# Reused bytes waited for tile by tile, and six row buffers instead of five

## The chip, the cores and the metric

The kernel runs on one core of one Trainium2 chip. The metric is device time of one execution in microseconds (us): 1251.45 before the change, the median of three runs (1250.16 to 1252.48). The core has five engines with a queue each, worked off in order: PE (TensorE, matmuls), DVE (VectorE), ACT (ScalarE), POOL (GpSimd) and SP (SyncE, which here only issues DMAs; POOL issues some too).

## The reference, cut to what matters

Attention over 4 batches, 8 heads, 576 tokens and a head width of 64, in which each query keeps its 32 largest scores; then a layer of eight experts (MoE), to which a token goes only if its skip score is positive, and there to one expert; then a gated layer over all 2304 tokens.

```
scores = q @ k.T / 8                       # 576 x 576 for each of 32 heads
kth = 32nd largest of each row;  scores = where(scores >= kth, scores, -1e9)
attn = softmax(scores) @ v                 # -> x, 2304 tokens x 512
do = x @ w_skip > 0                        # the tokens that are computed
e = argmax(x @ w_gate); p = softmax(x @ w_gate)[e]          # 8 experts
x[do] += p * (relu(x @ w1[e]) @ w2[e])     # w1: 512 x 1024, w2: 1024 x 512
g = x @ w_gate2;  v = x @ w_val            # 512 x 1536 each
out = (g * sigmoid(g) * v) @ w_out         # 1536 x 512
```

## The kernel before, in words

The four batches are worked in two groups of two (1152 tokens each). While the attention of the second group runs on DVE (MAX8 and MATCH_REPLACE find the 32 largest) and PE, the experts and the first part of the gated layer of the first group are mixed in. The attention's end at some 780 us is followed by the second group's experts, `moe1(1)`, mixed with the rest of the first group's gated layer `moe2(0)`, and at the end stands the gated layer of the second group, `moe2(1)`.

fp32 products are made of three matmuls on numbers split in a high and a low half. For the experts of the second group, `wsplit` loads 128x1024 weights (512 KB) into a buffer `wraw` (L947, on SP), ACT copies the high half into a buffer `whl` (L950), DVE subtracts it for the low half (L951), and PE multiplies three times (L1014 to L1016 for the first matrix of an expert, L1042 to L1044 for the second). Four `wraw` and six `whl` buffers go round (`Ring`). A row block of an expert is gathered from the rows `xa` by its list of indices (L960, a DMA of POOL) into a buffer `io`, turned on PE (L989), copied and split by ACT (L992) and DVE (L993), and behind the last output matmul added up and scattered back (L967). The result of the first matrix goes through ACT (`hn`, L1019) and is turned on PE again (L1025).

A gated block takes 384 tokens. For each of 12 units it needs 24 matmuls (L1146 to L1148); ACT and DVE or POOL make the gate of it (L1154 to L1158). Then 108 output matmuls follow (L1169 to L1171) into three banks of PSUM, which ACT copies to `io` buffers (L1175) from which SP stores them (L1177). Its weights come in split form from a scratch tensor `w2s` (L1108, POOL) or raw and are split on the fly (`wfly`: L1111 on SP, L1114 on ACT, L1115 on DVE or POOL). At a block's start three `io` buffers are loaded with rows (L1126) and turned (L1129), and split by ACT (L1131) and DVE (L1132).

The order on each engine is that in which a scheduler places the instructions of the program: it goes by the tiles' dependences, by the number of buffers of a name and by its own costs. Memory is handed out by pools, stacked from two sides. Two places matter here. At some 306 us the pool of the routing and first attention of group 0 closes, and `Moe`'s pools "moe" and "pm" open in its bytes; the first load there is L580, of gated weights into an `h2h` buffer, which DVE (L610 to L612) and others work on. At some 780 us `sa.close()` ends the attention's pools, and "moe2", "pm2" and "ring2" open in theirs; the first load there is L947. The routing of the second group ends with matmuls L547, which ACT copies (L550), and whose result gives the index lists.

The `Moe` object of the second pair has as its last argument the number of `io` buffers, 5, 128x512 floats each. They serve the gathers of `moe1(1)`, then the row loads and output copies of `moe2(1)`. The output copies of the first group's blocks have two `io` buffers of their own.

Of the kernel before, what the change touches and what calls it, by code (L numbers as in the profile page):

```python
# [32 lines left out]
class Kernel:  # L33
# [15 lines left out]
        self.constants()  # L49

    def pool(self, stack, name, side="left"):
        return stack.enter_context(self.tc.tile_pool(name=name, bufs=1, side=side))

    def psum_pool(self, stack, name, side="left"):
        return stack.enter_context(self.tc.tile_pool(name=name, bufs=1, side=side, space=bass.MemoryType.PSUM))

    def constants(self):
        nc, c = self.nc, self.const
# [388 lines left out]
    def rbank(self):  # L447
        if self.rps:
            pool, name, n = self.rps
            return pool.tile([P, 512], F32, name=name, bufs=n)  # L450
        return self.ps.tile([P, 512], F32, name="pT", bufs=3)
# [162 lines left out]
    def run(self):  # L614
        nc = self.nc
        with ExitStack() as st:
# [69 lines left out]
            while m1 and next(m1, None) is not None:  # L686
                pass
            sa.close()
            mp = Moe(self, self.pool(st, "moe2", "right"), self.psum_pool(st, "pm2", "right"), 5,
                     Ring(self.pool(st, "ring2", "right"), 4, 6), 5)  # L690
            n1 = mp.moe1(1, [nc.vector])
            while done2 < cost2 + PRE:
                done2 += next(m2)
# [232 lines left out]
class Moe:  # L926
    def __init__(self, k, pool, psum, nm, ring, nio):
        self.k, self.mo, self.nio = k, pool, nio
        self.ring = ring
        self.pm = self.po = psum  # L930
        self.nm = self.no = nm
        self.fly = None
        self.fresh = []
        self.io = pool
# [286 lines left out]
```

## Time and profile before

| | |
|---|---|
| median of three runs | 1251.45 us |
| the profiled execution: its own time | 1253.92 us |
| its span (first to last instruction) | 1252.1 us |
| PE busy | 1171.3 us, 94% |
| DVE busy | 987.5 us, 79% |
| ACT busy | 734.1 us, 59% |
| POOL busy | 595.0 us, 48% |
| mean granted clock of PE | 0.975 |

The profile is one execution. Busy time is a sum over the span; where an engine waits is seen in its timeline, which gives for each instruction its start, its length and, in brackets, the idle time before it with the event that ended it. The windows give busy times of stretches of 25 us.

### The profile page before, as it was taken

What the parts mean: (1) busy time and instruction counts of PE and PEld (TensorE: products, weight loads), DVE (VectorE), ACT (ScalarE), POOL (GpSimd) and SP (SyncE); (2) the same over time, 40 slices, a digit from 0 to 9 for tenths busy, and PEclk for the clock granted to TensorE, in tenths of its full rate; (3) what the DMA queues carried; (4) which work ended last, traced back from release to release, by engine and by line L of the source; (5) the groups of instructions that cost most, each with busy time, mean ns of one, the idle gap of its engine ahead of it and who ended that gap; (6) DMA issues with size and microseconds to landing.
All of it is one profiled execution on the core that took longest, in us unless ns stands there. A gap on an engine that the chain in (4) does not pass through costs nothing.

```text
span 1252.1 us, 21503 instructions
## 1 busy us (share of the span) xinstructions
PE 1171.3 (94%) x7253; PEld 1011.3 (81%) x7254; DVE 987.5 (79%) x2366; ACT 734.1 (59%) x1582; POOL 595.0 (48%) x770
## 2 busy tenths in 40 slices
PE   6999889999999999999988899889999999999995
PEld 5777777887687778878976798789988799898994
DVE  6999999999899999999999963168878257183670
ACT  5989888998655556555564533056766334343430
POOL 6778867887233435333562433212212535555540
PEclk9999999999798999999999999999999989999998
DMA  2023611111187988965756876778987534533520
GB/s 68 25 74 118 223 39 39 39 39 39 61 297 231 316 303 307 295 211 171 247 196 227 283 242 198 262 268 287 295 278 245 177 105 133 169 118 120 158 68 28
DMA packets 136797, 219.11 MB, mean 175 GB/s; under 512 B 37861, under 2 KB 95205, under 8 KB 130405
## 3 DMA queue, kind: packets, MB, share of 16 engines
q1 hardware_dynamic: 129652, 178.86, 43.7%
q0 software_dynamic: 7024, 38.78, 9.4%
q8 instruction: 59, 0.97, 0.3%
q14 instruction: 62, 0.50, 0.1%
HBM read 177.77 MB, written 41.95 MB: 175 GB/s over the span
## 4 chain that ended last, share of the span: by engine, by line
PE 43%; DVE 26%; DMA 9%; issue 4%; ACT 4%; POOL 1%; SPq 0%; ACTq 0%; DVEq 0%; POOLq 0%
PE m L1146 7%; PE m L1147 7%; PE m L1148 7%; DVE tops L255 7%; DVE rest L254 6%; DMA wraw<-in_moe_w_dram 5%; PE m L1092 3%; PE m L1170 3%; PE m L1171 3%; PE m L1169 2%; PE m L1079 2%; PE pT L290 2%; DVE whl L951 2%; PE pT L276 2%; PE pS L207 2%
## 5 line engine op out<-in xcount | busy, mean ns | idle before, releaser
L255 DVE MAX8 tops<-rest 128x8 f32<-128x288 f32 (+1 forms) x432 | 229.8, 546 | 1.6
L1146 PE MATMUL m<-x2h,whl 128*128 128x384 f32 x576 | 198.5, 346 | 11.7 <-ACT io L1175 7.0
L1147 PE MATMUL m<-x2l,whl 128*128 128x384 f32 x576 | 196.6, 341 | 0.9 <-DVE x2l L1132 0.9
L1148 PE MATMUL m<-x2h,whl 128*128 128x384 f32 x576 | 196.0, 341 | 0.0
L1115 POOL TENSOR_TENSOR whl<-wfly,whl 128x1024 fp32r<-128x1024 f32 x54 | 130.1, 2410 | 116.3 <-ACT whl L1114 116.3
L1114 ACT ACTIVATE whl<-wfly 128x1024 fp32r<-128x1024 f32 x69 | 73.1, 1061 | 110.8 <-PE m L1148 65.3
L278 ACT ACTIVATE pt<-pT 128x512 f32<-128x512 f32 (+2 forms) x320 | 113.6, 405 | 41.3 <-PE pT L276 39.8
L254 DVE MATCH_REPLACE8 rest<-tops,rest 128x288 f32<-128x288 f32 x288 | 125.8, 438 | 0.0
L1146 PEld LDWEIGHTS m<-x2h,whl 128*128 128x128 f32 x576 | 109.9, 191 | 14.9 <-ACT io L1175 7.8
L276 PE MATMUL pT<-idn,pp 128*128 128x128 f32 (+1 forms) x720 | 115.1, 284 | 6.3 <-DVE pp L259 4.8
L951 DVE TENSOR_TENSOR whl<-wraw,whl 128x1024 fp32r<-128x1024 f32 x64 | 82.4, 1304 | 39.8 <-ACT whl L950 32.3
L1147 PEld LDWEIGHTS m<-x2l,whl 128*128 128x128 f32 x576 | 109.7, 190 | 1.8 <-DVE x2l L1132 1.2
L1148 PEld LDWEIGHTS m<-x2h,whl 128*128 128x128 f32 x576 | 109.3, 190 | 0.4 <-issue 0.2
L217 ACT ACTIVATE sc<-pS 128x576 f32<-128x576 f32 x144 | 93.5, 649 | 23.8 <-PE pS L207 18.4
L207 PE MATMUL pS<-kT,qT 128*128 128x288 f32 x512 | 104.9, 326 | 2.6 <-ACT sc L217 1.0
L1158 DVE TENSOR_TENSOR h2l<-th,h2h 128x384 fp32r<-128x384 f32 x36 | 86.3, 2396 | 23.9 <-ACT h2h L1157 23.9
L1158 POOL TENSOR_TENSOR h2l<-th,h2h 128x384 fp32r<-128x384 f32 x36 | 45.7, 1270 | 112.8 <-ACT h2h L1157 112.7
L276 PEld LDWEIGHTS pT<-idn,pp 128*128 128x128 f32 (+1 forms) x720 | 83.3, 140 | 17.4 <-issue 10.8
L950 ACT ACTIVATE whl<-wraw 128x1024 fp32r<-128x1024 f32 x64 | 66.8, 1056 | 48.0 <-DMA wraw<-in_moe_w_dram 40.9
L1155 DVE SCALAR_TENSOR_TENSOR th<-th,m 128x384 f32<-128x384 f32 x72 | 39.1, 543 | 68.7 <-ACT th L1154 68.7
L1169 PE MATMUL m<-whl,h2h 128*128 128x512 f32 x216 | 85.7, 401 | 0.8 <-ACT whl L589 0.8
L290 PE MATMUL pT<-pt,vv 128*64 128x256 f32 (+1 forms) x512 | 81.7, 437 | 5.0 <-ACT pt L278 4.9
(205 smaller groups left out, 2935.3 us busy)
## 6 DMA issues: line engine op xcount, KB each, us to landing
wfly<-w2s SPq DMA_DIRECT2D x69, 512.0 KB, 3.6
whl<-in_moe_w_dram SPq DMA_DIRECT2D x32, 1024.0 KB, 7.7
wraw<-in_moe_w_dram SPq DMA_DIRECT2D x64, 512.0 KB, 5.0
whl<-w2s POOLq DMA_DIRECT2D x31, 1024.0 KB, 5.5
w2s<-h2h SPq DMA_DIRECT2D x8, 1024.0 KB, 6.2
w2s<-whl SPq DMA_DIRECT2D x8, 1024.0 KB, 11.0
io<-xa SPq DMA_DIRECT2D x18, 256.0 KB
out_dram<-io SPq DMA_DIRECT2D x18, 256.0 KB, 2.0
```

What stands on the lines that cost most here:

```text
L207: m = self.nc.tensor.matmul(pS[:, x, :W], l, r[:, x * W:(x + 1) * W], start=(n == 0), stop=stop and n == len(ops) - 1)
L254: self.mark = nc.vector.match_replace(hj, h[:, (j - 1) * 8:j * 8], hi if j == 1 else hj, NEG)
L255: nc.vector.max(h[:, j * 8:(j + 1) * 8], hj if j < 3 else rest.rearrange("p a b -> p (a b)"))
L276: self.anchor = nc.tensor.transpose(p[:k, c - a, :], pp[:, c * P:c * P + k], self.idn)
L278: nc.scalar.activation(T[:k, a:z, do:do + n], p[:k, :z - a, so:so + n], AF.Copy)
L951: lo_engine.tensor_tensor(lo, raw, hi.bitcast(F32), op=OP.subtract)
L1115: self.fly_engine.tensor_tensor(lo, raw, hi.bitcast(F32), op=OP.subtract)
L1146: nc.tensor.matmul(pz, wh[:, z, k, :], xh[:, k, :], start=(k == 0), stop=False)
L1147: nc.tensor.matmul(pz, wh[:, z, k, :], xl[:, k, :], start=False, stop=False)
L1148: nc.tensor.matmul(pz, wl[:, z, k, :], xh[:, k, :], start=False, stop=(k == 3))
L1158: lo_engine.tensor_tensor(hl[:, f, :], th, hh[:, f, :].bitcast(F32), op=OP.subtract)
L1169: nc.tensor.matmul(po[t], hh[:, f, s], wh[:, k, :], start=(f == 0), stop=False)
```

## The change

Both helper functions that make pools get an argument: `reuse_waits="tile"`. Without it, the first instruction that uses bytes of a closed pool waits for all that used that pool; with it, for those that used the tiles whose bytes it takes. And the second `Moe` object has six `io` buffers instead of five. The new line in the second helper moves every later line number by one: L947 before is L948 after.

```
--- before.py
+++ after.py
@@ -49,10 +49,11 @@
         self.constants()
 
     def pool(self, stack, name, side="left"):
-        return stack.enter_context(self.tc.tile_pool(name=name, bufs=1, side=side))
+        return stack.enter_context(self.tc.tile_pool(name=name, bufs=1, side=side, reuse_waits="tile"))
 
     def psum_pool(self, stack, name, side="left"):
-        return stack.enter_context(self.tc.tile_pool(name=name, bufs=1, side=side, space=bass.MemoryType.PSUM))
+        return stack.enter_context(self.tc.tile_pool(name=name, bufs=1, side=side, space=bass.MemoryType.PSUM,
+                                                     reuse_waits="tile"))
 
     def constants(self):
         nc, c = self.nc, self.const
@@ -687,7 +688,7 @@
                 pass
             sa.close()
             mp = Moe(self, self.pool(st, "moe2", "right"), self.psum_pool(st, "pm2", "right"), 5,
-                     Ring(self.pool(st, "ring2", "right"), 4, 6), 5)
+                     Ring(self.pool(st, "ring2", "right"), 4, 6), 6)
             n1 = mp.moe1(1, [nc.vector])
             while done2 < cost2 + PRE:
                 done2 += next(m2)
```

With the argument alone the order of instructions is unchanged on every engine, and only waits differ. SP at the second pair of pools, before (`wraw`, `wfly`: weight loads; the names in brackets are what is waited for, DMAHW a lane of DMAs):

```order
L947 DMA wraw<-in_moe_w_dram 128x4x256 [waits DMAHW3_49,DMAHW1_49,DMAHW6_49,DMAHW0_49,DMAHW7_49,PE_49,Pool_49]
L1111 DMA wfly<-w2s 128x1024 [waits DMAHW5_49]
L947 DMA wraw<-in_moe_w_dram 128x4x256 x3
L1111 DMA wfly<-w2s 128x1024
L1111 DMA wfly<-w2s 128x1024 [waits DMAHW2_49]
L947 DMA wraw<-in_moe_w_dram 128x2x512 [waits DMAHW4_49,DVE_49]
L947 DMA wraw<-in_moe_w_dram 128x2x512 [waits DMAHW6_49,DVE_49]
```

and after:

```order
L948 DMA wraw<-in_moe_w_dram 128x4x256
L1112 DMA wfly<-w2s 128x1024 [waits DMAHW5_49]
L948 DMA wraw<-in_moe_w_dram 128x4x256 [waits DMAHW6_49]
L948 DMA wraw<-in_moe_w_dram 128x4x256 [waits DMAHW7_49]
L948 DMA wraw<-in_moe_w_dram 128x4x256 [waits DMAHW0_49]
L1112 DMA wfly<-w2s 128x1024 [waits DMAHW1_49]
L1112 DMA wfly<-w2s 128x1024 [waits DMAHW2_49]
L948 DMA wraw<-in_moe_w_dram 128x2x512 [waits DMAHW4_49,DMAHW3_49,DVE_49]
L948 DMA wraw<-in_moe_w_dram 128x2x512 [waits DMAHW6_49,DVE_49]
```

The order is the same; the first load lost its waits for PE, POOL and five lanes, and the next loads got waits for one lane each.

The sixth buffer moves instructions behind the second pair of pools. SP at the end of the experts, before (`io<-xa`: row loads of a gated block; `out_dram<-io`: stores of outputs):

```order
L1111 DMA wfly<-w2s 128x1024 x4
L1126 DMA io<-xa_214 128x512 x3
L1111 DMA wfly<-w2s 128x1024 x2
L1126 DMA io<-xa_214 128x512
L1111 DMA wfly<-w2s 128x1024
L1126 DMA io<-xa_214 128x512
L1111 DMA wfly<-w2s 128x1024
L1177 DMA out_dram<-io 128x512 x2
L1126 DMA io<-xa_214 128x512
L1177 DMA out_dram<-io 128x512
```

and after:

```order
L1112 DMA wfly<-w2s 128x1024 x5
L1127 DMA io<-xa_214 128x512 x3
L1112 DMA wfly<-w2s 128x1024
L1127 DMA io<-xa_214 128x512 x3
L1112 DMA wfly<-w2s 128x1024 x2
L1178 DMA out_dram<-io 128x512 x3
```

The six row loads stand three and three, all ahead of the first store, and one `wfly` load has moved ahead of the first three.

PE at the second matrix of the first of these experts, before (L1042 to L1044: that matrix; L1146 to L1148: the gated layer):

```order
L1148 MATMUL m<-x2h,whl 128x384
L1043 MATMUL m<-whl,hh 128x512
L1044 MATMUL m<-whl,hl 128x512
L1042 MATMUL m<-whl,hh 128x512
L1043 MATMUL m<-whl,hh 128x512
L1044 MATMUL m<-whl,hl 128x512
L1042 MATMUL m<-whl,hh 128x512
L1043 MATMUL m<-whl,hh 128x512
L1044 MATMUL m<-whl,hl 128x512
L1042 MATMUL m<-whl,hh 128x512
L1146 MATMUL m<-x2h,whl 128x384
L1147 MATMUL m<-x2l,whl 128x384
```

and after:

```order
L1149 MATMUL m<-x2h,whl 128x384
L1044 MATMUL m<-whl,hh 128x512
L1045 MATMUL m<-whl,hl 128x512
L1147 MATMUL m<-x2h,whl 128x384
L1148 MATMUL m<-x2l,whl 128x384
L1149 MATMUL m<-x2h,whl 128x384
L1147 MATMUL m<-x2h,whl 128x384
L1148 MATMUL m<-x2l,whl 128x384
L1149 MATMUL m<-x2h,whl 128x384
L1147 MATMUL m<-x2h,whl 128x384
L1148 MATMUL m<-x2l,whl 128x384
L1149 MATMUL m<-x2h,whl 128x384
```

Twelve gated matmuls have moved ahead of seven matmuls of the expert. On POOL six gathers (L960) stand in a row at the start of these experts instead of five, ahead of the same two `whl` loads, and the one that stood behind the first scatter is gone from there.

## Rows read from the trace of the kernel before

**Rows 1.** Windows: from:to, us, busy (x) of PE PEld DVE ACT POOL, clock, DMA share, GB/s.
```profile
775.00:800.00 25.00, 22.68 (x130) 18.91 (x129) 7.81 (x48) 2.75 (x8) 6.41 (x10) 0.93 0.58 193
800.00:825.00 25.00, 17.12 (x79) 14.47 (x78) 8.09 (x9) 8.25 (x11) 3.70 (x5) 0.86 1.03 361
...
850.00:875.00 25.00, 25.00 (x165) 23.85 (x164) 22.09 (x24) 16.98 (x24) 6.17 (x4) 1.00 0.89 290
```

**Rows 2.** Timeline of PE, 807 to 824: start, length, engine, line, operation, [idle before].
```profile
807.71 0.60 PE L989 MATMUL m<-idn,io 128*128 128x128 f32 x4
812.98 0.69 PE L1146 MATMUL m<-x2h,whl 128*128 128x384 f32 x1 [4.67 <-ACT io L1175]
...
816.66 0.52 PE L1148 MATMUL m<-x2h,whl 128*128 128x384 f32 x1
819.55 0.44 PE L1146 MATMUL m<-x2h,whl 128*128 128x384 f32 x1 [2.37 <-ACT io L1175]
...
821.57 0.34 PE L1148 MATMUL m<-x2h,whl 128*128 128x384 f32 x1
...
823.50 0.39 PE L1016 MATMUL m<-whl,xg 128*128 128x256 f32 x1 [0.82 <-DVE xg L993]
```

**Rows 3.** Timeline of ACT, 795 to 821.
```profile
795.77 0.18 ACT L550 ACTIVATE r_first<-pT 128x16 f32<-128x16 f32 x1 [13.54 <-PE pT L547]
802.04 1.06 ACT L950 ACTIVATE whl<-wraw 128x1024 fp32r<-128x1024 f32 x1 [6.08 <-DMA wraw<-in_moe_w_dram]
811.38 1.06 ACT L950 ACTIVATE whl<-wraw 128x1024 fp32r<-128x1024 f32 x1 [8.28 <-DMA wraw<-in_moe_w_dram]
812.35 0.58 ACT L1175 ACTIVATE io<-m 128x512 f32<-128x512 f32 x1
817.96 1.06 ACT L950 ACTIVATE whl<-wraw 128x1024 fp32r<-128x1024 f32 x1 [5.03 <-DMA wraw<-in_moe_w_dram]
...
820.35 1.05 ACT L950 ACTIVATE whl<-wraw 128x1024 fp32r<-128x1024 f32 x1
```

**Rows 4.** Timeline of SP, 778 to 800: DMAs it issues.
```profile
778.81 0.57 SPq L434 DMA_DIRECT2D xa<-x  x1
795.80 0.39 SPq L947 DMA_DIRECT2D wraw<-in_moe_w_dram  x1
...
796.79 2.62 SPq L947 DMA_DIRECT2D wraw<-in_moe_w_dram  x3
```

**Rows 5.** Waits of SP, 775 to 824: us in total, times, longest.
```profile
SPq L947 <- PE pT L547: 13.3, 1, 13.3
```

**Rows 6.** Timeline of DVE, 803 to 823.
```profile
803.13 1.23 DVE L951 TENSOR_TENSOR whl<-wraw,whl 128x1024 fp32r<-128x1024 f32 x1 [6.90 <-DMA wfly<-w2s]
...
822.76 0.68 DVE L993 TENSOR_TENSOR xg<-m,xg 128x512 fp32r<-128x512 f32 x1
```

**Rows 7.** Timelines of ACT and PE, 950 to 953.
```profile
950.89 1.06 ACT L950 ACTIVATE whl<-wraw 128x1024 fp32r<-128x1024 f32 x1 [4.66 <-DMA wraw<-in_moe_w_dram]
...
952.49 0.66 PE L1025 MATMUL m<-idn,hn 128*128 128x128 f32 x4 [1.56 <-ACT hn L1019]
```

**Rows 8.** Waits of SP, 300 to 345.
```profile
SPq L580 <- PE pT L276: 28.6, 1, 28.6
```

**Rows 9.** Timelines of ACT and DVE near 342.
```profile
342.31 0.66 ACT L217 ACTIVATE sc<-pS 128x576 f32<-128x576 f32 x1
...
343.00 1.36 DVE L610 TENSOR_SCALAR h2h<-h2h 128x1024 int32<-128x1024 int32 x1 [2.38 <-PE pT L300]
```

**Rows 10.** Timeline of POOL near 803.
```profile
803.14 0.61 POOL L1108 DMA_DIRECT2D whl<-w2s  x1
```

**Rows 11.** Timelines of SP, ACT and PE, 998 to 1005.
```profile
998.94 0.86 SPq L1177 DMA_DIRECT2D out_dram<-io  x2
...
1003.26 0.60 ACT L1175 ACTIVATE io<-m 128x512 f32<-128x512 f32 x1 [3.31 <-DMA out_dram<-io]
...
1004.40 1.01 PE L1146 MATMUL m<-x2h,whl 128*128 128x384 f32 x2 [4.70 <-ACT x2h L1131]
```

More of the change, by code (lines that the diff above doesn't have):

```diff
@@ L51, in pool @@
     def pool(self, stack, name, side="left"):
-        return stack.enter_context(self.tc.tile_pool(name=name, bufs=1, side=side))
+        return stack.enter_context(self.tc.tile_pool(name=name, bufs=1, side=side, reuse_waits="tile"))
     def psum_pool(self, stack, name, side="left"):
-        return stack.enter_context(self.tc.tile_pool(name=name, bufs=1, side=side, space=bass.MemoryType.PSUM))
+        return stack.enter_context(self.tc.tile_pool(name=name, bufs=1, side=side, space=bass.MemoryType.PSUM,
+                                                     reuse_waits="tile"))
     def constants(self):
@@ L689, in run @@
             mp = Moe(self, self.pool(st, "moe2", "right"), self.psum_pool(st, "pm2", "right"), 5,
-                     Ring(self.pool(st, "ring2", "right"), 4, 6), 5)
+                     Ring(self.pool(st, "ring2", "right"), 4, 6), 6)
             n1 = mp.moe1(1, [nc.vector])
```

## The prediction

> **What bounds the kernel now.** I read the 25 us windows first, then the engines' timelines in the windows where TensorE (PE) is not full, then the waits of SP's queue, whose loads stand at the start of those gaps. In most windows of the second half PE is busy for all of its 25 us at a granted clock of 1.00 (850 to 875 in [rows 1]); nothing but less PE work or less waiting helps there. The exception is 800 to 825: PE busy 17.12, clock 0.86, while the DMA share is 1.03 at 361 GB/s, after a window with 193 GB/s [rows 1]. Here the second group's experts begin. In [rows 2] the reader is to see PE end the gated output at 807.71 and a turn of 0.60, then stand idle for 4.67 until ACT's copy L1175, run twelve gated matmuls whose starts lie 3.68 us apart first to last (812.98 to 816.66), wait 2.37 for the next copy, run twelve in 2.02 (819.55 to 821.57), and wait 0.82 for DVE's L993 before the first L1016 at 823.50. [Rows 3] say why: the copy at 812.35 stands in ACT's order behind the split L950 of 811.38, which waited 8.28 us for a `wraw` load; the third split waited 5.03 more. [Rows 4, 5] say why the loads are late: SP issues nothing between 778.81 + 0.57 and 795.80, since the first `wraw` waits 13.3 us for PE's last routing matmul L547. It reads and writes nothing that this load touches: the load goes into bytes of the attention's pool, which was closed just before, and the wait is for all who used that pool.
>
> **The change part by part, against the profiled execution** (span 1252.1, its own time 1253.92, which is 2.47 above the median of 1251.45; what is saved in the span is taken off the median).
>
> 1. *Waits of the second pair of pools.* By the order with waits, the first `wraw` load now waits for nothing, and the six loads behind it only for DMA lanes whose last users (row loads and stores up to 778.81, [rows 4]) landed long before 795. So four `wraw` and three `wfly`, each 128x1024 floats, 0.52 MB, can issue from 779.4 instead of 795.80: 3.67 MB. At 361 GB/s [rows 1] that is 10.2 us, so all land by about 790; if they get only what the old window left over (361 - 193 = 168 GB/s), the fourth `wraw`, fifth in the queue, 2.6 MB, lands by 795. Either is in time for what follows.
> ACT is in order, and its routing copy L550 at 795.77 [rows 3] stays ahead of the splits, since it still waits for PE. Then splits 1 and 2 run at 796 to 798 without a wait. L1175 needs a finished output bank, at the latest 807.71, the end of the output on PE [rows 2]. From there ACT's in-order chain, by durations: copy 0.58, split three 1.06, copy 0.58, a conversion of `wfly` that is the same work as a split, 1.06, split four 1.05 [rows 3]: 812.04. Then DVE's L951 of split four, 1.23, and L993, 0.68 [rows 6]: 813.95; starts overlap by about 0.1 at each handover (811.38 + 1.06 against 812.35), so about 813.5. PE meanwhile: the turn ends at 808.31; from 819.55 to 823.50, less its wait of 0.82, the second twelve and the few matmuls behind them take 3.13; the first twelve at that speed take 2.02 and one interval more, 2.20: 808.31 + 5.33 = 813.6. Between 813.5 and 813.95 I take 813.8, against 823.50: **9.7 us** less. What is late next is split four with L993, by a few tenths. The two ends of this term: 6.0, if only the first split moves (802.04 to 796) and each later one keeps its distance; 9.9, if PE alone sets it (813.6).
> Is the gain kept? PE's later windows are full, but the weight stream runs beside it at nearly its own pace, and [rows 7] show one place where it already overtakes: ACT waited 4.66 for a `wraw`, and hn behind it held PE for 1.56. There is a second such place near 913. The stream starts earlier by what PE does: split 3 gives its raw buffer back about 10 us sooner, so loads 7 and 8 stand as far ahead of PE as before, and 5 and 6 farther. I leave both stalls as they are.
>
> On the slow twelve: the row shows that right after the 4.67 us stop PE's matmuls start at intervals of 0.335 against 0.184 later [rows 2], with a granted clock of 0.86 over that window [rows 1]. The Trainium skill, page "TensorE: Matmul & The Clock Gate", section "HAM oscillation — how this bites in real kernels", says that a stop in which PE waits for data lets the clock fall to half, so the next group starts cold. By that rule the 1.66 us goes with the stop, as I count it; without it the sum would be 8.0 for this term.
>
> 2. *Waits of the first pair of pools.* SP stands for 28.6 us before L580 for PE [rows 8]; now only a DMA lane is left. The weights come early, and DVE's stop of 2.38 before L610 at 343.00 [rows 9], in a stretch where DVE is the full engine, can go. But the next DVE work there, L221, needs ACT's scores, ready at 342.31 + 0.66 = 342.97: L610 takes 1.36 and used up the wait; of its time no more than 1.3 can be gained by moving it into the hole. Bounds 0 to 1.3, I take **0.7**.
>
> 3. *Waits added.* The new waits name producers that ended long ago. 0.
>
> 4. *Six row buffers.* POOL issues six gathers in a row before the two `whl` loads at 803.14 [rows 10] instead of five: about 1.25 later, the distance of two gathers. PE needs those loads only for the gated step behind the first half of expert 0, near 820, so the cover is some 10 us. On PE, groups of gated matmuls change places with output matmuls of the experts from the first expert on; they are the same matmuls, in windows where PE is full: 0, bounds -3 to +5 (two stalls of 1.56 fewer; three more).
>
> 5. *The stop at 999 to 1004.* The third output copy waits 3.31 for the first output's DMA, and PE 4.70 behind it [rows 11]. Those two buffers are not the ones that grow. SP's `wfly` load now stands ahead of three row loads and not behind them, so the conversion ahead of the output's issue can start sooner. Bounds -1 to +2, I take **1.0**.
>
> Sum: 9.7 + 0.7 + 1.0 = 11.4, so 1253.92 - 11.4 = 1242.5 as the profiled execution would read, and 1251.45 - 11.4 = **1240.0** as the median. With the bounds of the terms: from 6.0 + 0 - 1 = 5.0 to 9.9 + 1.3 + 2 + 3 (the stalls of part 4) = 16.2, that is 1246.5 to 1235.2; the loss in part 4 has a rival of its own.
>
> **A rule that speaks against part 1.** The row first: in the crowded window the splits come 9.3 and 6.6 us apart, though SP had issued the first four `wraw` loads by 799.4 [rows 3, 4]. The Trainium skill, "DMA: Bandwidth & Descriptors", section "Queues, rings and completion order", says that each DMA engine alternates between the queues that have work, packet by packet. By it the early loads would share each engine with POOL's queue while that has loads of its own (a DMA share of 0.58 over 775 to 800, [rows 1]); they would take twice the 10.2 us at most, 20.4, and the last would land at 800. The splits that PE waits for come after 807, so the forecast would stand.
>
> **The rivals.**
> - *Only the first split moves* (chance 0.14). For: the second and third splits also have in front of them copies that wait for PE, and loads still meet gathers at 797 to 803. Against: all seven loads precede the gathers by 17 us. Gain 6.0 + 0.7: 1244.7.
> - *The stream of weights takes part back* (0.12): PE, 10 us ahead, meets stalls such as 1.56 [rows 7] at three more experts, 4.7: 1244.7 again, by another way. For: ACT and DVE reach 17 to 22 of 25 us there [rows 1]. Against: the stream starts as much earlier.
> - *More than counted* (0.10): the two stalls at 913 and 952 go as well, 3.1, and the stop at 999 shrinks by 2: 1235.9.
> - *It does not do what it says* (0.06): some wait other than the pool's holds SP or ACT, for instance L550, which ACT's order puts ahead of the splits. Then 795.77 remains the start of everything, splits 1 and 2 move and the rest is as crowded as before: 1250 to 1251.
> - *Slower* (0.05): the new order with six row buffers puts ACT's L950, waiting for a load, ahead of hn in the five experts where it does not now stand so, and all of its wait of 4.66 [rows 7] reaches PE each time: 5 x 4.66 = 23.3, less 11.4: 1263. It decides from 2.8 us an expert on (five times that is 11.4 + 2.5). Against: PE then would have to be out of work in windows that are full, and the measured part of such a wait that came through was 1.56.
>
> **How the numbers follow.** The forecast itself has 0.53. About 0.2%, 2.5 us, is what a measurement of this kernel can tell from no change. Faster: 0.53 + 0.14 + 0.12 + 0.10 = 0.89; the same 0.06; slower 0.05. The range runs from the case "more" to the two partial cases and the lower bound of the terms, with a little over for the run itself: 1235.0 to 1247.0.
>
> **What would show it.** Right: SP's first `wraw` near 779.5, splits 1 and 2 at 796 to 798, no stop of PE between 808 and 813, the first L1016 near 814, the clock of that window near 1.00. Part 2: L580 near 307 and DVE's stop at 343 smaller. Part 5: PE's stop near 990 below 4.70. Wrong: PE out of work in the experts' windows at more than two places, or the first split after 800.

## The result, and the profile after

The changed kernel takes 1239.7 us (median of 6 runs, 1237.89 to 1241.29) against 1250.82 for the kernel before in the same runs (6, 1249.09 to 1257.58): a ratio of 0.9902, 95% interval 0.9878 to 0.9926, or 11.1 us. Measured again beside other kernels it was 1237.2 against 1251.26, ratio 0.9878 (0.9855 to 0.9900). The forecast was 11.4 us and 1240.0. The profiled execution took 1237.89, its span is 1236.0 us: 16.1 less than the span before. This pair of traces thus shows more than the medians do; the kernel before was profiled 3.1 us above its median in those runs, the changed one 1.8 below. (Line numbers of the changed kernel are one higher than before; in e3, e4 and e5 they are two higher, in e7 three, in e9 the same.)

The windows of the changed kernel, with the columns of [rows 1]:

```profile
775.00:800.00 25.00, 22.76 (x131) 19.15 (x130) 10.18 (x50) 4.65 (x10) 7.17 (x10) 0.93 0.95 330
800.00:825.00 25.00, 25.00 (x155) 23.34 (x154) 10.66 (x13) 11.79 (x18) 5.57 (x7) 1.00 0.88 317
```

Both answer to rows of before: 800 to 825 had 17.12 us of PE at clock 0.86, and now has 25.00 at 1.00, while the window ahead of it moves 330 GB/s instead of 193. The loads have moved by a window, and no stop is left in the one where they were. SP's timeline, to be read beside [rows 4]:

```profile
778.87 0.57 SPq L435 DMA_DIRECT2D xa<-x  x1
779.49 0.63 SPq L948 DMA_DIRECT2D wraw<-in_moe_w_dram  x1
780.17 0.98 SPq L1112 DMA_DIRECT2D wfly<-w2s  x1
781.19 1.79 SPq L948 DMA_DIRECT2D wraw<-in_moe_w_dram  x3
783.03 1.80 SPq L1112 DMA_DIRECT2D wfly<-w2s  x2
```

The first `wraw` load follows the row store at once, at 779.49 instead of 795.80, and all seven loads are issued by 784.8. As far as the trace shows their landing, the `wraw` loads land 6.5 to 8.5 us after issue and the three `wfly` loads 9.0 to 9.4, so the last by 793.6, before ACT can use them. ACT, beside [rows 3]:

```profile
795.61 0.18 ACT L551 ACTIVATE r_first<-pT 128x16 f32<-128x16 f32 x1 [12.93 <-PE pT L548]
795.69 2.00 ACT L951 ACTIVATE whl<-wraw 128x1024 fp32r<-128x1024 f32 x2
806.38 0.60 ACT L1176 ACTIVATE io<-m 128x512 f32<-128x512 f32 x1 [8.69 <-PE m L1172]
806.88 1.05 ACT L951 ACTIVATE whl<-wraw 128x1024 fp32r<-128x1024 f32 x1
807.83 0.59 ACT L1176 ACTIVATE io<-m 128x512 f32<-128x512 f32 x1
808.30 1.06 ACT L1115 ACTIVATE whl<-wfly 128x1024 fp32r<-128x1024 f32 x1
809.25 1.06 ACT L951 ACTIVATE whl<-wraw 128x1024 fp32r<-128x1024 f32 x1
```

Splits 1 and 2 come right behind the routing copy (x2 at 795.69) with no wait for data. The output copies L1176 and splits 3 and 4 stand back to back from 806.38 to 810.3. PE, beside [rows 2]:

```profile
807.55 0.60 PE L990 MATMUL m<-idn,io 128*128 128x128 f32 x4
807.90 0.42 PE L1147 MATMUL m<-x2h,whl 128*128 128x384 f32 x1
...
812.00 0.34 PE L1149 MATMUL m<-x2h,whl 128*128 128x384 f32 x1
...
812.65 0.28 PE L1017 MATMUL m<-whl,xg 128*128 128x256 f32 x1
```

The gated matmuls begin 0.35 us behind the start of the turn and run through; the last of the 24 starts at 812.00, and the first L1017 (L1016 before) at 812.65 instead of 823.50, with no idle time ahead of it.

### The profile page after: what moved, and what is told of

It reads as the page before. It is cut to its first block, busy times and chain, and to the rows that moved or that the text cites. A ratio compares the mean times of both kernels' runs of the same rounds, so it can differ in the third digit from the quotient of the medians.

```text
span 1236.0 us, 21482 instructions
## 1 busy us (share of the span) xinstructions
PE 1166.1 (94%) x7253; PEld 1008.5 (82%) x7254; DVE 984.0 (80%) x2366; ACT 733.0 (59%) x1582; POOL 600.0 (49%) x770
## 4 chain that ended last, share of the span: by engine, by line
PE 54%; DVE 15%; DMA 5%; issue 4%; ACT 2%; POOL 1%; SPq 0%; DVEq 0%; POOLq 0%; ACTq 0%
PE m L1147 7%; PE m L1149 7%; PE m L1148 7%; DVE tops L256 4%; DVE rest L255 4%; PE m L1171 4%; PE m L1172 4%; PE m L1170 4%; PE m L1093 3%; PE m L1080 3%; PE pT L291 2%; PE pS L208 2%; PE pT L277 2%; DVE rest L248 1%; DVE pp L260 1%
## 5 line engine op out<-in xcount | busy, mean ns | idle before, releaser
L1148 PE MATMUL m<-x2l,whl 128*128 128x384 f32 x576 | 195.4, 339 | 0.0
L1148 PEld LDWEIGHTS m<-x2l,whl 128*128 128x128 f32 x576 | 108.7, 189 | 0.6 <-issue 0.2
L952 DVE TENSOR_TENSOR whl<-wraw,whl 128x1024 fp32r<-128x1024 f32 x64 | 78.8, 1246 | 26.9 <-ACT whl L951 26.6
L208 PEld LDWEIGHTS pS<-kT,qT 128*128 128x128 f32 x512 | 78.9, 199 | 10.6 <-ACT sc L218 3.3
```

Source lines behind the costliest of these rows:

```text
L208: m = self.nc.tensor.matmul(pS[:, x, :W], l, r[:, x * W:(x + 1) * W], start=(n == 0), stop=stop and n == len(ops) - 1)
L1148: nc.tensor.matmul(pz, wh[:, z, k, :], xl[:, k, :], start=False, stop=False)
```

## Experiments

All times are medians, with the ratio to the kernel before, measured beside it, and its 95% interval. The ratio is not the quotient of the two medians; here the two differ by up to 0.002. e1 to e4 ran on one chip, e5 to e11 on another, each group beside runs of the kernel before. In the traces I measure two stretches of PE: A, from the start of the turn of the second group's first expert (L989, 807.71 in the kernel before) to the first L1016, and B, from there to the first gated matmul behind the stop near 1000 (1004.40). Each holds the same number of matmuls in every kernel, 32 and 1048. What stands ahead of A moves by several us between executions (the turn starts between 796.9 and 811.1), so I compare stretches and not times of day.

| kernel | waits by tile | buffers, first and second pair | A, us | B, us | ratio |
|---|---|---|---|---|---|
| before | none | 2, 5 | 15.79 | 180.90 | 1 |
| changed | all | 2, 6 | 5.10 | 176.56 | 0.9902 (0.9878 to 0.9926) |
| changed, again | all | 2, 6 | 5.08 | 175.74 | 0.9878 (0.9855 to 0.9900) |
| e1 | all | 2, 5 | 5.09 | 179.37 | 0.9916 (0.9889 to 0.9944) |
| e2 | none | 2, 6 | 17.47 | 177.54 | 1.0001 (0.9981 to 1.0020) |
| e3 | second pair | 2, 6 | 5.08 | 177.27 | 0.9917 (0.9889 to 0.9946) |
| e4 | ring2 alone | 2, 6 | 14.62 | 179.30 | 0.9960 (0.9934 to 0.9985) |
| e5 | first pair | 2, 5 | 17.11 | 178.97 | 0.9977 (0.9951 to 1.0004) |
| e6 | all, stores from ACT | 2, 6 | 5.08 | 173.72 | 0.9826 (0.9796 to 0.9856) |
| e7 | all, third copy to the second pair's buffers | 2, 6 | 5.09 | 180.85 | 0.9910 (0.9883 to 0.9936) |
| e8 | all | 3, 5 | 5.35 | 175.09 | 0.9791 (0.9763 to 0.9820) |
| e9 | none | 3, 5 | 17.08 | 175.30 | 0.9916 (0.9894 to 0.9938) |
| e10 | all, stores from ACT | 3, 5 | 5.35 | 176.07 | 0.9820 (0.9788 to 0.9852) |

**e1: the waits alone.** Against the changed kernel:

```
-                     Ring(self.pool(st, "ring2", "right"), 4, 6), 6)
+                     Ring(self.pool(st, "ring2", "right"), 4, 6), 5)
```

> Tile-wise waits in all pools, five row buffers as before. Theory A (the waits at the second pair of pools are the whole gain): the stop of TensorE behind the first group's last output is gone as in the changed kernel, first L1016 of the experts 10 to 11 us earlier than before, the two stalls on hn near 913 and 950 and the stop of 4.7 us at the end of the experts stay in some form; time 10 to 11 us below the kernel before, ratio 0.991 to 0.992. Theory B (the sixth buffer gives a good part, by its new order): the same gain at the start, but 3 to 5 us of the changed kernel's gain are missing, ratio 0.994 to 0.995.

Measured: 1239.25 against 1251.89. Its PE rows (the turn, the longer of two stalls on hn, the stop at the end of the experts):

```profile
800.37 0.60 PE L990 MATMUL m<-idn,io 128*128 128x128 f32 x4
...
933.29 0.66 PE L1026 MATMUL m<-idn,hn 128*128 128x128 f32 x4 [1.91 <-ACT hn L1020]
...
984.83 1.65 PE L1147 MATMUL m<-x2h,whl 128*128 128x384 f32 x4 [4.19 <-ACT x2h L1132]
```

A is as short as in the changed kernel, and the stalls on hn and the stop of 4.19 us are still there, as theory A has it. The ratio, 0.9916, cannot be told from the changed kernel's; the 3 to 5 us that would be missing by theory B are not seen in it.

**e2: the sixth buffer alone.** The change without `reuse_waits="tile"` in both helpers.

> Six row buffers, waits as before. Theory A: the stops at 808 to 824 stay as before (4.7, 2.4 and 0.8 us), time within 1 us of before, ratio 0.999 to 1.000. Theory B: the stalls on hn near 913 and 950 go and the stop at the end of the experts shrinks, 3 to 5 us below before, ratio 0.996 to 0.997. If the new order cost something that the waits made good: over 1.001.

Measured: 1250.79 against 1251.89, ratio 1.0001. PE:

```profile
807.49 0.60 PE L990 MATMUL m<-idn,io 128*128 128x128 f32 x4
814.43 0.69 PE L1147 MATMUL m<-x2h,whl 128*128 128x384 f32 x1 [6.34 <-ACT io L1176]
...
820.90 0.69 PE L1147 MATMUL m<-x2h,whl 128*128 128x384 f32 x1 [2.27 <-ACT io L1176]
...
1002.50 1.65 PE L1147 MATMUL m<-x2h,whl 128*128 128x384 f32 x4 [5.67 <-ACT x2h L1132]
```

The stop behind the turn is 6.34 us, the second 2.27, the one at the end 5.67. The stalls on hn are gone, as the new order would have it, but stretch A is 1.7 us longer than before, and the time is the same within 0.2%. This is what theory A expects. The four `wraw` loads, issued from 795.58 on, take 16.2 to 22.9 us to land where the trace shows it, against 6.5 to 8.5 in the changed kernel: held back, they run beside the gathers and loads of POOL.

**e3: the second pair alone.** `reuse_waits="tile"` only for the pools moe2, pm2 and ring2 (cut to the line that both helpers get).

```
+        kw = dict(reuse_waits="tile") if name in ('moe2', 'pm2', 'ring2') else dict()
```

> Six row buffers, tile-wise waits only in the three pools of the second pair (moe2, pm2, ring2); the first pair waits as before, SP's 28 us wait for L580 near 307 to 336 included. Theory A: as the changed kernel, ratio 0.990 to 0.991, DVE stops 2.4 us near 343 but loses nothing of it by 720. Rival C (the first pair is worth the 0.7 us of the sum, up to 1.3): 0.7 us slower than the changed kernel, and DVE's work between 350 and 720 later by as much.

Measured: 1240.07 against 1251.89, 0.9917. The second pair's waits are enough. Now the first pair's place: in e3, L582 (L580 before) is issued at 334.03, nearly as late as before (335.70). DVE:

```profile
339.23 0.69 DVE L612 TENSOR_SCALAR h2h<-h2h 128x1024 int32<-128x1024 int32 x1 [0.29 <-POOL L L442]
340.89 0.46 DVE L223 TENSOR_TENSOR hi<-sc,pS 128x288 f32<-128x288 f32 x1 [0.97 <-ACT sc L219]
```

and in the changed kernel, where the same load is issued 28 us earlier than before (SP, the longest wait of SP between 300 and 345, and DVE):

```profile
307.44 0.44 SPq L581 DMA_DIRECT2D h2h<-in_moe_w_gate_dram  x1
...
SPq L122 <- PE pT L277: 29.8, 1, 29.8
...
340.07 0.87 DVE L611 TENSOR_SCALAR h2h<-h2h 128x1024 int32<-128x1024 int32 x1
340.86 0.43 DVE L222 TENSOR_TENSOR hi<-sc,pS 128x288 f32<-128x288 f32 x1
```

With the load late, DVE waits 0.29 ahead of L612 here, 2.32 in e2's trace, 1.97 in e4's, 0.25 in e9's and 2.38 in [rows 9]; with the load early it does not wait there in any (changed kernel twice, e1, e5 to e8, e10). But in e5 and e7 it then stops one instruction later, for ACT's scores:

```profile
340.91 0.45 DVE L223 TENSOR_TENSOR hi<-sc,pS 128x288 f32<-128x288 f32 x1 [2.14 <-ACT sc L219]
```

This is e5; e7 has 2.15 there. So the stop ahead of the load's first use is real, of a size that varies, and goes, but in two of eight traces a stop of 2.1 us stands right behind it. And SP's queue stands as long as before: L122, the next load, now waits 29.8 us for PE in place of L580's 28.6 [rows 8].

**e4: only the first load free.** `reuse_waits="tile"` for ring2 alone. The first `wfly`, from the pool moe2, waits as before, and three `wraw` loads stand behind it.

> As the second-pair kernel, but tile-wise waits only in the pool of the weight ring: the first wraw load waits for nothing and is early, the first wfly load behind it in SP's queue still waits for the routing's last matmul, and with it the three other wraw and two wfly loads. Theory A (the splits three and four decide, which need the whole group of loads early): split one at 796, but the third copy-blocking split still near 811 to 818, gain 0 to 3 us beside what the six buffers give, ratio 0.996 to 1.000. Rival D (the first load's start decides, each later one keeps its distance): 6 us below before, ratio 0.994 to 0.996.

Measured: 1245.25 against 1251.89, 0.9960, with single runs from 1238.69 to 1252.33. SP, ACT and PE in the profiled execution, which at 1252.33 is the slowest of its runs:

```profile
780.07 0.62 SPq L949 DMA_DIRECT2D wraw<-in_moe_w_dram  x1
796.18 0.33 SPq L1113 DMA_DIRECT2D wfly<-w2s  x1
796.56 2.18 SPq L949 DMA_DIRECT2D wraw<-in_moe_w_dram  x3
...
796.22 1.05 ACT L952 ACTIVATE whl<-wraw 128x1024 fp32r<-128x1024 f32 x1
806.05 1.06 ACT L952 ACTIVATE whl<-wraw 128x1024 fp32r<-128x1024 f32 x1 [8.77 <-DMA wraw<-in_moe_w_dram]
...
819.74 1.06 ACT L952 ACTIVATE whl<-wraw 128x1024 fp32r<-128x1024 f32 x1 [7.61 <-DMA wraw<-in_moe_w_dram]
...
808.09 0.60 PE L991 MATMUL m<-idn,io 128*128 128x128 f32 x4
...
821.34 0.58 PE L1016 MATMUL m<-whl,xg 128*128 128x256 f32 x1 [7.73 <-ACT xg L994]
```

Split 1 is at 796.22, as theory A and D both have it. Split 4 waits till 819.74 and PE 7.73 us behind it, so A is 14.62, a gain of 1.2. The ratio says 5 us, the trace 1.2, and the runs span both. Of the two theories the trace of the longest run is for A; the ratio is at the edge of both. How the loads fare in the shorter runs no trace shows; this stays open. In this trace, at least, the first load alone does not give what the seven give: the three `wraw` loads issued from 796.56 on take 9.3 to 21.7 us to land. In time, 9 of its 12 runs are longer than the longest of e3 (1242.56), but the two intervals overlap.

**e5: the first pair alone**, five buffers, `reuse_waits="tile"` for moe and pm.

> Five row buffers, tile-wise waits only in the first pair's pools (moe, pm). Theory A: L580's weights come 28 us earlier and DVE's stop near 343 shrinks, but what DVE gains there it has lost again by 720 (it waits for TensorE and for gathers on the way); ratio 0.999 to 1.001. Rival C: the 0.7 us of the sum, up to 1.3, are kept: ratio 0.9990 to 0.9995, DVE still 0.7 to 1.3 us earlier at 720.

Measured: 1249.12 against 1253.21, 0.9977; the interval holds 1, and the ratio itself lies below what either theory expected. DVE in its trace is 1.6 us earlier than before at 322, 2.4 earlier at 362, 1.3 later at 402 and 2.4 earlier at 724: no offset that stays. The 1.6 at 322 stand ahead of the place where the change can act. In time this is inconclusive; if there is a gain, no trace shows where it is.

**e6: stores from ACT's queue.** Against the changed kernel:

```
-                nc.sync.dma_start(self.out[r:r + P, :], ot)
+                nc.scalar.dma_start(self.out[r:r + P, :], ot)
```

> The changed kernel with the stores of the outputs issued from ACT's queue, right behind the copy that fills the buffer, instead of from SP's, where weight loads stand ahead of them. If the stop of TensorE near 985 (4.0 us; the third copy waits for the first store) is made by the queue: the store lands 2 to 2.5 us after its copy instead of 4.9, the stop shrinks to 1.5 to 2, ratio 0.988 to before. If it is made by the DMA engines, which are full of weight loads whoever issues: no change, 0.990.

Measured: 1231.43 against 1253.21, 0.9826, more than I expected, and not by the way I expected. First the changed kernel at that place (SP, ACT, PE, answering to [rows 11]):

```profile
983.17 5.86 SPq L1178 DMA_DIRECT2D out_dram<-io  x3
...
982.54 1.28 ACT L1176 ACTIVATE io<-m 128x512 f32<-128x512 f32 x2 [5.78 <-PE m L1172]
...
988.07 0.60 ACT L1176 ACTIVATE io<-m 128x512 f32<-128x512 f32 x1 [2.65 <-DMA out_dram<-io]
...
989.21 0.97 PE L1147 MATMUL m<-x2h,whl 128*128 128x384 f32 x4 [4.03 <-ACT x2h L1132]
...
991.28 0.52 PE L1147 MATMUL m<-x2h,whl 128*128 128x384 f32 x1
991.60 0.52 PE L1148 MATMUL m<-x2l,whl 128*128 128x384 f32 x1
```

then e6 (ACT, with its DMA issues, and PE):

```profile
978.16 1.28 ACT L1176 ACTIVATE io<-m 128x512 f32<-128x512 f32 x2 [4.82 <-PE m L1172]
978.90 0.91 ACTq L1178 DMA_DIRECT2D out_dram<-io  x2
979.96 1.57 ACT L1132 ACTIVATE x2h<-m 128x512 fp32r<-128x512 f32 x3 [0.52 <-PE m L1130]
985.43 0.60 ACT L1176 ACTIVATE io<-m 128x512 f32<-128x512 f32 x1 [3.90 <-DMA out_dram<-io]
...
981.58 0.97 PE L1147 MATMUL m<-x2h,whl 128*128 128x384 f32 x4 [0.79 <-ACT x2h L1132]
```

The store is not faster: issued at 978.90, it lets the third copy go only at 985.43. But in e6's order the copies of the turn, L1132, stand ahead of that third copy and not behind it, so PE waits 0.79 instead of 4.03. Both of my readings of the stop (SP's queue or the DMA engines) missed that the copy's place in ACT's order hands the wait on. The gated matmuls behind the stop change too: they start 0.32 us apart in the changed kernel and 0.18 apart in e6 (983.16 to 983.34), with a granted clock of 0.93 and 1.00 over 975 to 1000. Of the 8.5 us by which e6's span is shorter than the changed kernel's, B and what follows it hold 3.7. The other 4.8 stand ahead of A, where traces of the same instructions differ by more than that (the turn starts at 807.55 and 811.14 in the changed kernel, at 800.37 in e1, which differs only in the second pair's buffers), so what e6 does there is not shown.

**e7: a third buffer for the last copy**, from the six of the second pair (the edit cut to the lines that choose the buffer).

```
+                sb3, n3 = (self.third, 6) if t == 2 and self.third is not None else (self.io, self.nio)
+                ot = sb3.tile([P, D], F32, name="io", bufs=n3)
```

> The changed kernel, but the third output copy of the first group's last block goes to one of the six row buffers of the second pair, so that it waits for no store. The row loads of the next block then stand behind the first store in SP's queue. Theory: the wait of the third copy goes, and TensorE waits for the row loads in its place, 1.5 to 2.5 us instead of 4.0; ratio 0.988 to 0.989. Rival: the loads take as long as the store did, 4 us, no gain, 0.990.

Measured: 1241.25 against 1253.21, 0.9910 (0.9883 to 0.9936). PE:

```profile
979.40 0.65 PE L1132 MATMUL m<-idn,io 128*128 128x128 f32 x4 [2.87 <-DMA io<-xa]
984.23 1.94 PE L1132 MATMUL m<-idn,io 128*128 128x128 f32 x8 [4.17 <-DMA io<-xa]
986.86 1.65 PE L1149 MATMUL m<-x2h,whl 128*128 128x384 f32 x4 [0.69 <-ACT x2h L1134]
```

This is the rival: PE waits 2.87 and 4.17 for the row loads, which now stand behind the store. The wait has changed its name and has not shrunk.

**e8: three and five buffers**, `..., 3, ring, 3)` for the first pair and 5 for the second, with the waits by tile (the argument ahead of the last bracket was 2 for the first pair).

> The changed kernel with three row buffers in the first pair and five in the second (there is no room for three and six). The stop near 777 (2.2, a row load that waits for one of two buffers) and that near 985 (4.0) should both go: 5 to 6 us below the changed kernel, ratio 0.985 to 0.986 to before. Rival: the third buffer changes how experts and attention are mixed from 340 on, and this costs as much as it saves: 0.990 or more.

Measured: 1226.39 against 1253.21, 0.9791: 26.8 us below the kernel before. ACT and PE:

```profile
973.87 1.96 ACT L1176 ACTIVATE io<-m 128x512 f32<-128x512 f32 x3 [6.29 <-PE m L1172]
975.72 1.57 ACT L1132 ACTIVATE x2h<-m 128x512 fp32r<-128x512 f32 x3
...
977.35 0.96 PE L1147 MATMUL m<-x2h,whl 128*128 128x384 f32 x4 [0.84 <-ACT x2h L1132]
```

All three copies run at once, and PE waits 0.84. The stop near 777 (2.24 in the changed kernel) is gone as well. By its median this is the fastest kernel of the study, and the gain over the changed kernel, 11 to 14 us by the ratios, is about twice what I expected. The trace's span is 13.0 shorter than the changed kernel's. A, B and what follows hold 2.4 of it; the other 10.6 stand ahead of A, and of these the stop near 777 is 2.24. With three buffers in the first pair the turn starts at 796.91 (e8), 801.27 (e10) and 802.60 (e9), with two anywhere from 800.37 to 811.14. How much of the rest is the third buffer's is thus not shown.

**e9: three and five buffers with the old waits.**

> Three and five row buffers, but the waits for reused bytes by whole pools, as in the kernel before. If the two edits work at different places (waits at 808 to 824, third buffer at 777 and 985), their gains add: this kernel 15 to 16 us below before (27 of the three-and-five kernel less 11), ratio 0.987 to 0.988, with TensorE's stops of 4 to 5 and 2 to 3 us behind the output there again. Rival: the third buffer alone brings it, the early loads nothing beside it: ratio 0.979 to 0.981.

Measured: 1240.62 against 1251.26, 0.9916, so 10.6 us, less than the 15 to 16 that I expected. PE:

```profile
802.60 0.60 PE L989 MATMUL m<-idn,io 128*128 128x128 f32 x4
807.14 0.55 PE L1146 MATMUL m<-x2h,whl 128*128 128x384 f32 x1 [3.94 <-ACT io L1175]
...
814.82 0.69 PE L1146 MATMUL m<-x2h,whl 128*128 128x384 f32 x1 [3.77 <-ACT io L1175]
```

The stops behind the turn are back, 3.94 and 3.77 us, and A is 17.08. The two edits work at different places: by the medians their gains are 10.6 and 11.1 to 14.1, together 21.7 to 24.7, against 26.8 for both. Whether the 2 to 5 us between are more than noise is not shown. The rival, that the third buffer alone brings the gain, is out.

**e10: e8's buffers and e6's stores together.**

> Three and five row buffers with tile-wise waits, and the outputs stored from ACT's queue. Both edits act on the same stop near 985, which is 0.8 us with either; so nothing beyond the three-and-five kernel, ratio 0.978 to 0.980. Rival: stores from ACT's queue also free SP's queue elsewhere: 0.975 or less.

Measured: 1229.47 against 1251.26, 0.9820. There is no gain beyond e8, as expected; the ratio is a little above the 0.978 to 0.980 that I gave, PE waits 1.45 at the stop instead of 0.84, and the intervals of both kernels overlap.

**e11: the changed kernel again.**

> The changed kernel itself, on the chip of the two others: 11 us below before, ratio 0.990 to 0.992.

Measured: 1237.2 against 1251.26, 0.9878, a little more gain than expected.

## Why the prediction was right

- *The number.* 11.4 us against 11.1, and against 14.1 in the second measurement; both medians lie in the range. That the first comes so near is in part luck: part 1 gave 1.0 more than counted, and the 1.7 of parts 2 and 5 cannot be seen in the times.
- *Part 1, 9.7 us: right in mechanism and nearly in size.* A fell from 15.79 to 5.10, by 10.7, over the upper bound of 9.9. The bound has 5.93 us from the start of the turn to the first L1017, and 5.10 were measured. It took the end of the turn as its row's start and length, 808.31, but PE's rows overlap, and the next matmul started 0.35 after the turn's start (807.55 to 807.90); and it took the few matmuls behind the 24 from a stretch that a stop had broken, 1.11, where they take 0.65 (812.00 to 812.65). ACT was no limit: I had its first copy wait till 807.71 at the latest, and it ran at 806.38, so split 4 began at 809.25, and its low half and L994 were done at 812.35, 0.3 us before PE needed them. Here PE alone set the first L1017, but by little: in e8 L994 ends at 802.20, the first L1017 follows at 802.26, and A is 5.35. e1 and e3 show that the waits of the second pair make all of it, and e2 that the buffers make none.
- *The clock* went as the rows of before showed: without the 4.67 us stop there are no slow twelve; the window's granted clock is 1.00 instead of 0.86. The changed kernel's own stop of 4.03 at 989.21 is again followed by slow gated matmuls, 0.32 us apart from 990.6 to 993.8, and in e6, where that stop is 0.79, they are 0.18 apart.
- *The rule held against part 1.* It had the last of the seven loads land by 800. They landed by 793.6, and POOL's three loads beside them took 7.2 to 7.7 us instead of 5.2 to 5.8. This cost PE no stop: it is busy for all of 785 to 795 and of 795 to 805.
- *Is the gain kept?* Yes. B did not grow in any kernel with an early start.
- *Part 2, 0.7 us: not shown.* The stop goes, but its size is 0.25 to 2.38 in the traces that have the wait, in e5 and e7 the wait for ACT's scores takes its place (2.14 and 2.15), and DVE's lead of 3.6 us at 355 in the changed kernel is gone by 720 (0.04 at 704). e3, which keeps the wait, is as fast as the changed kernel within the intervals. If 0.7 us is there, it is below what these runs can tell.
- *Parts 4 and 5, together 1.0 us: too low beside the traces.* B is 4.3 us shorter in the changed kernel. Between traces with two buffers in the first pair and six in the second (177.54, 177.27, 176.56, 175.74, 179.30; e6 and e7, which change the stop itself, left out) and with two and five (180.90, 179.37, 178.97) the means differ by 2.5 us. The stalls on hn (1.67 and 1.56 before) are gone, with 0.39 near 939 in the changed kernel; the case "more than counted" had this. The stop at the end fell from 4.70 to 4.03. In the times none of it can be seen: neither in e1 against the changed kernel nor in e2, at 1.0001.
- *The rivals.* "Only the first split moves" was tried on its own in e4: 1.2 us in the trace, 5 by the ratio, which is not far from the 6.0 of that rival. The changed kernel's rows are against it all the same, since splits 3 and 4 run there without a wait for data. A stream of weights that takes the gain back, no effect, and a loss do not appear in any trace.

## What to carry to other kernels

Where a queue of loads stands still at the change from one phase to the next, ask whether the wait belongs to the bytes or to the pool: the price is not that wait but the collision of all the loads that it lets go at once (16.2 to 22.9 us to land in e2, 6.5 to 8.5 in the changed kernel), read at the engine that copies and splits them in order. After this gain the next stop was an in-order engine whose early instruction waits for a buffer and holds a later one that somebody needs; a buffer more (e8) or another place in the order (e6) took it away, in e6 though the transfer was no faster. And the size of a stop is known only when a second execution has it too: one and the same was 0.25 to 2.38 us here.

## What the runs showed of the hardware

A store of an output buffer (128x512 floats) issued from ACT's queue took no less time to free that buffer than one from SP's, in one execution of each: 978.90 to 985.43 in e6, 983.17 to 988.07 in the changed kernel.

Loads of 512 KB issued one behind the other from 779.49 on landed in 6.5 to 9.4 us (changed kernel); issued from 795.58 on, together with gathers and loads of POOL's queue, `wraw` loads took 16.2 to 22.9 (e2).

Behind the stops of 4.67 us (before) and 4.03 us (changed kernel), 128x384 matmuls started 0.33 and 0.32 us apart; behind that of 0.79 us (e6), 0.18 apart.
